# One core, attention, feed-forward and expert slots in one kernel: lower weight parts on GpSimd, fixed probability buffers, and a new order at slots 0 and 1

## The chip, the core and the metric

One core of a Trainium2 chip runs the whole kernel; the metric is the time of one execution on the device in microseconds. The engines are named as the profile names them: PE (TensorE, matmuls; PEld its weight loads), DVE (VectorE), ACT (ScalarE), POOL (GpSimd) and SP (SyncE, which here mostly issues transfers).

## The reference

Three stages follow each other. B=4, H=8, S=576, D=64, so there are 2304 tokens of width 512.

```python
scores = scale * np.matmul(q, k.transpose(0, 1, 3, 2))
scores = np.where(masks, scores, -1e9)          # heads 0-3 local (32 back), 4-7 strided by 32
attn = np.exp(scores - scores.max(-1, keepdims=True))
attn = attn / (attn.sum(-1, keepdims=True) + 1e-09)
x = (attn @ v) as rows of 512
xn = x / np.sqrt(np.mean(x * x, -1) + 1e-6) * rms_g
g = xn @ w_gate                                  # 512 -> 1536
x = (g * sigmoid(g) * (xn @ w_val)) @ w_out      # 1536 -> 512
e = argmax(x @ router + modality_bias[modality_id])
out = prob[e] * (relu(x @ w1[e]) @ w2[e])        # one of 8 experts a token, 512 -> 1024 -> 512
```

## The kernel before, in words

**Attention.** The work is cut into 48 units, 12 for each batch; unit u is two heads by a group of two to four tiles of queries. `attention(u, banks)` gives a unit four steps: `scores` (two matmuls a tile, then on DVE the scaled and masked scores go from PSUM into the SBUF tile `pr`, L207, and the row minimum is taken, L215; ACT takes the exponentials in place, L218), `norm` (DVE: row sum L238, reciprocal, product L242), `transpose` (PE L248, ACT copy L250) and `output` (PE L259). The first 12 units, those of batch 0, run alone at the start. In them the sum takes one column more than the probabilities, which holds 1e-9: GpSimd sets it in each unit (L185). The tile `pr` comes from a pool of three.

**Feed-forward.** Tokens are taken in nine chunks of 256. Before chunk 0 can start, its rows are squared and summed (L368 to L382), a reciprocal root is made on DVE (L388 to L396), and the normalised rows are split (L414 to L418). Every product is made of three matmuls, with both operands split into an upper and a lower part (`gate_val`, L512 to L514; `ff_out`, L537 to L539). The weights are 36 pieces of 128 by 512. They come as raw pairs of words, on ACT's transfer queue, and are made into two parts in three steps:

- `conv_a(n)`: GpSimd casts 16 bits of each word into one of two halves of `top` (L453);
- `conv_b(n)`: DVE shifts the other word and puts both together (L457);
- `conv_c(n)`: ACT rounds the result to the upper part (L464), DVE subtracts that from it for the lower part (L465).

The list `conv` holds the steps in the order a(0), b(0), a(1) with c(0), b(1), a(2) with c(1), and so on; `convert` takes them up while attention still runs. A scheduler with a simulated timeline sets each engine's order in this part of the program, so an edit can also move instructions that it doesn't name.

**Experts.** A router (`routes`, `route_i` for the last step of a chunk: four matmuls at L678 and one sum into `ids`) ranks the tokens of each expert. Slots of up to 256 tokens follow, each with one expert. `find`, `whose` and `count` work out which token columns and which expert each slot has; this is done at once for slots 1 and 2 (`SOON` is 2) and later for 13 more. For a slot t, `gather(t)` makes indices on DVE (L1046 to L1055) and issues two gathers of rows on POOL (L1058); `experts(t)` and `load` let SP fetch the expert's weights; `split(i)` halves them into upper (ACT L1074) and lower parts (DVE L1075); `x_transpose` puts the rows on PE (L1089) and splits them (L1093, L1094); `mm1` (L1110 to L1112) has four groups of two halves, `relu_split` makes `hT` (DVE L1127), `mm2` (L1140 to L1142) gives the output, and `finish(t)` scales it to `y` (DVE L1171 for its first half) and issues two scattered writes on POOL (L1172). This part stands in the order that the program gives (`manual_schedule`): slot 0 is written out by hand around the routing of the last chunk, and `run(1, BASE)` loops over the slots behind it.

Of the kernel before, what the change touches and what calls it, by code (L numbers as in the profile page):

```python
# [10 lines left out]
F32 = mybir.dt.float32  # L11
# [7 lines left out]
ALU = mybir.AluOpType  # L19
AX = mybir.AxisListType  # L20
# [33 lines left out]
def moe_kernel(  # L54
# [50 lines left out]
    pp = p_att.enter_context(tc.tile_pool(name="pp", bufs=4))  # L105
    xt_p = p_att.enter_context(tc.tile_pool(name="xt", bufs=4))

    def bank(tag, bufs=1):
        return ps.tile([128, 512], F32, tag=tag, name=tag, bufs=bufs)

# [61 lines left out]
    def attention(u, banks):  # L172

        b, p, g = units[u]
        local = p < 2
        n, t0, nq, nk = geometry(u)
        k0 = n * nq if local else n * nq + LQ - SQ
        st = {}

        def scores():  # L180
            t = qkv_t.pop((u, 0))

            pr = pp.tile([128, 4, LK + 1], F32, tag="pr", name="pr", bufs=3)
            if u < 12:
                G.memset(pr[:, :n, nk:nk + 1], 1e-9)  # L185
            mx = sm.tile([128, 4], F32, tag="mx", name="mx")
            sd = sm.tile([128, 4], F32, tag="sd", name="sd")
            sps = banks("s")
            if 0 < u < 12:
                fill(sps[:, 384:], 10)  # L190
            sps = sps[:, :4 * LK].rearrange("p (t k) -> p t k", k=LK)
            with close_to(pv_last):
                for i in range(n):
                    for h in range(2):
                        hp = slice(64 * h, 64 * h + 64)
                        T.matmul(
                            sps[hp, i, :nk],
                            t[hp, i * nq:i * nq + LQ],
                            t[hp, k0 + i * nq:k0 + i * nq + nk],
                            start=True,  # L200
                            stop=True,
                        )
            pv_last[0] = None
            first = 1 if local and g == 0 else 0
            for i0, i1, mask in ((0, first, m_loc0), (first, n, m_loc if local else m_str)):
                if i1 > i0:
                    V.scalar_tensor_tensor(  # L207
                        out=pr[:, i0:i1, :nk],
                        in0=sps[:, i0:i1, :nk],
                        scalar=-0.125,  # L210
                        in1=mask[:, :nk].unsqueeze(1).to_broadcast([128, i1 - i0, nk]),
                        op0=ALU.mult,
                        op1=ALU.add,
                    )
            V.tensor_reduce(out=mx[:, :n], in_=pr[:, :n, :nk], op=ALU.min, axis=AX.X)  # L215
            for i in range(n):
                pv = pr[:, i, :nk]
                act = A.activation(  # L218
                    out=pv,
                    in_=pv,  # L220
                    func=AF.Exp,
                    bias=mx[:, i:i + 1],
                    scale=-1.0,
                    accum_out=None if u < 12 else sd[:, i:i + 1],
                )
                if not flow_on:
                    mark[0] = act
            st["p"] = pr, sd
            if not 3 <= u < 6:
                load_part(0)  # L230
            if u < 4:
                load_part(1)

        def norm():
            pr, sd = st["p"]
            pv, sl = pr[:, :n, :nk], sd[:, :n]
            if u < 12:
                V.tensor_reduce(out=sl, in_=pr[:, :n, :nk + 1], op=ALU.add, axis=AX.X)  # L238
            else:
                V.tensor_scalar(out=sl, in0=sl, scalar1=1e-9, scalar2=None, op0=ALU.add)  # L240
            V.reciprocal(out=sl, in_=sl)
            V.tensor_tensor(out=pv, in0=pv, in1=sl.unsqueeze(2).to_broadcast([128, n, nk]), op=ALU.mult)  # L242

        def transpose():
            pr, _ = st.pop("p")
            pt = banks("t").rearrange("p (t k) -> p t k", k=128)
            for i in range(n):
                T.transpose(pt[:nk, i], pr[:, i, :nk], ident)  # L248
            ptS = st["t"] = pp.tile([128, 4, 128], F32, tag="ptS", name="ptS", bufs=2)
            A.copy(ptS[:nk, :n], pt[:nk, :n])  # L250

        def output():
            t = qkv_t.pop((u, 1))
            ptS = st.pop("t")
            ot = banks("o")
            with close_to([None]):
                for i in range(n):
                    for h in range(2):
                        pv_last[0] = T.matmul(  # L259
                            ot[64 * h:64 * h + 64, i * nq:(i + 1) * nq],  # L260
                            t[:nk, i, 64 * h:64 * h + 64],
                            ptS[:nk, i, 64 * h:64 * h + nq],
                            start=True,
                            stop=True,
                        )
            if local:
                x = x_t[b, p, g] = xt_p.tile([128, n * LQ], F32, tag=f"x{g}", name=f"x{g}", bufs=2)
                A.copy(x, ot[:, :n * LQ])
            else:
                if g == 0:  # L270
                    x_t[b, p] = xt_p.tile([128, S], F32, tag="xs", name="xs", bufs=4)
                x = x_t[b, p].rearrange("p (j c) -> p c j", c=CLS)
                c0, c1 = 3 * t0, min(3 * (t0 + n), CLS)
                A.copy(x[:, c0:c1], ot[:, :(c1 - c0) * LEN].rearrange("p (c j) -> p c j", j=LEN))
            if not 2 <= u < 8:
                load_part(1)
            n_out[0] = u + 1


        if local and b > 0:  # L280
            output.after = (S * (b - 1) + LQ * (t0 + n) - 1) // CH
        elif not local and b > 1:
            output.after = (S * (b - 1) - 1) // CH
        return scores, norm, transpose, output
# [176 lines left out]
    def conv_c(n):  # L461
        wk = raw_t.pop(n)[:, :, 0].bitcast(F32)
        w = w_t[n] = w_slot(n, [128, 2, 512], F32R, "wf")
        A.copy(w[:, 0], wk)  # L464
        V.tensor_tensor(out=w[:, 1], in0=wk, in1=w[:, 0].bitcast(F32), op=ALU.subtract)  # L465

    n_wl = [0]
    mark = [None]
# [784 lines left out]
    def run(t0, t1, first=False):  # L1253
# [9 lines left out]
                x_transpose(t0, q)  # L1263
        for t in range(t0, t1):
            ahead = t + 1 < t1
            if t + 2 < t1:
                gather(t + 2)
            if t - 1 in ys:
                finish(t - 1)
            ef = experts(t + 2) if ahead else None  # L1270
            if t == BASE - 1:
                half_pair(t, 0)
# [32 lines left out]
    with tc.manual_schedule():  # L1305
# [11 lines left out]
            next(ranks)  # L1317
        weave(ranks, route_g(j), tables())
        mm1(0, 2, (1,))
        mm1(0, 3, (0,))  # L1320
        route_i(j)
        mm1(0, 3, (1,), relu=False)
        gather(1)
        mm2(0, 0)
        weave(whose(0, SOON))
# [14 lines left out]
        for i in range(3, 7):  # L1340
            split(i)
        split(7)
        weave(find(SOON, NL))
        weave(whose(SOON, NL), count())
        ef = experts(2)
        for i in range(8):
            load(ef, i)
# [108 lines left out]
```

## Time and profile before

| | |
|---|---|
| median of three runs | 843.76 us (842.97 to 846.24) |
| the profiled execution | 844.88 us |
| its span | 843.0 us |
| granted TensorE clock, mean | 0.987 |
| busy PE / DVE / ACT / POOL | 820.0 / 520.6 / 381.5 / 88.1 us |

The span runs from the first to the last instruction in the trace; 1.9 us of the execution lie around it. A busy time is the sum of an engine's records, and records of one engine can overlap a little where an instruction starts before the one ahead has drained. The stretch up to about 46 us is attention of batch 0, with the first weight pieces; from there to 590 us the feed-forward runs, with attention of the other batches woven in; behind it come the expert slots.

### The profile page before, as it was taken

Reading aid. Unit: us, or ns where it says so; the run is one execution under the profiler, and the core shown is the slowest. Engines: PE = TensorE matmul, PEld = TensorE weight load, DVE = VectorE, ACT = ScalarE, POOL = GpSimd, SP = SyncE. Lnnn points to the kernel's source line nnn. Section 1 sums busy time; section 2 is a strip of 40 time slices with the busy share of each in tenths; the row PEclk is TensorE's granted clock in tenths of the full one; section 3 lists DMA queues with packets and bytes.
Section 4 is the critical chain, followed back from the end, with each engine's and each line's share of the span. In section 5 each row is a group of like instructions: output and inputs, shape, how many; then the busy total and the mean of one; then the engine's idle time right before and its main releaser. Section 6 shows DMA issues by size and latency. Waiting matters only on the chain.

```text
span 843.0 us, 17634 instructions
## 1 busy us (share of the span) xinstructions
PE 820.0 (97%) x6746; PEld 741.6 (88%) x6746; DVE 520.6 (62%) x1444; ACT 381.5 (45%) x943; POOL 88.1 (10%) x103
## 2 busy tenths in 40 slices
PE   8699999999999999999999999999999999999996
PEld 7588988988988998899989999999898999999995
DVE  5979994454663564653554525538589666666762
ACT  5756564343454345443242322325265555455552
POOL 2414410000000000000000000001023112221201
PEclk9879999999999999999999999999999999999998
DMA  9959301111211111200000000005159777777773
GB/s 249 365 190 344 107 25 34 29 34 39 63 57 43 38 34 51 76 23 1 26 11 26 1 1 27 1 26 214 37 175 338 224 225 229 217 232 230 230 222 111
DMA packets 35587, 96.99 MB, mean 115 GB/s; under 512 B 4786, under 2 KB 12322, under 8 KB 35496
## 3 DMA queue, kind: packets, MB, share of 16 engines
q1 hardware_dynamic: 26520, 67.08, 25.6%
q10 hardware_dynamic: 5616, 19.07, 6.1%
q0 software_dynamic: 3360, 9.64, 3.4%
q8 instruction: 55, 0.90, 0.4%
q14 instruction: 36, 0.29, 0.1%
HBM read 91.04 MB, written 9.71 MB: 120 GB/s over the span
## 4 chain that ended last, share of the span: by engine, by line
PE 77%; DVE 9%; issue 7%; DMA 4%; ACT 1%; POOL 1%; SPq 1%; POOLq 0%; DVEq 0%; ACTq 0%
PE gv L512 11%; PE gv L513 11%; PE gv L514 11%; PE o L538 5%; PE o L537 5%; PE o L539 5%; PE o L1140 3%; PE o L1142 3%; PE o L1141 3%; PE s L1110 2%; DVE raw L457 2%; PE s L1111 2%; PE s L1112 2%; PE mx L259 2%; DVE wf L465 2%
## 5 line engine op out<-in xcount | busy, mean ns | idle before, releaser
L512 PE MATMUL gv<-xh,wf 128*128 128x256 f32 x864 | 246.9, 287 | 0.6 <-DVE t L522 0.3
L513 PE MATMUL gv<-xl,wf 128*128 128x256 f32 x864 | 245.6, 285 | 0.3
L514 PE MATMUL gv<-xh,wf 128*128 128x256 f32 x864 | 245.0, 284 | 0.0
L512 PEld LDWEIGHTS gv<-xh,wf 128*128 128x128 f32 x864 | 163.4, 190 | 7.2 <-issue 1.2
L513 PEld LDWEIGHTS gv<-xl,wf 128*128 128x128 f32 x864 | 163.7, 189 | 5.0 <-DVE xl L418 0.9
L514 PEld LDWEIGHTS gv<-xh,wf 128*128 128x128 f32 x864 | 163.9, 190 | 0.5 <-issue 0.2
L1075 DVE TENSOR_TENSOR l<-stg,h 128x1024 fp32r<-128x1024 f32 x88 | 107.1, 1224 | 34.1 <-ACT h L1074 33.9
L1074 ACT CAST h<-stg 128x1024 fp32r<-128x1024 f32 x88 | 91.5, 1047 | 30.8 <-PE o L1142 14.5
L521 DVE SCALAR_TENSOR_TENSOR t<-t,gv 128x256 f32<-128x256 f32 x108 | 45.1, 418 | 85.8 <-ACT t L520 85.0
L520 ACT ACTIVATE t<-gv 128x256 f32<-128x256 f32 x108 | 41.1, 381 | 122.5 <-PE gv L514 111.7
L525 ACT CAST hh<-t 128x256 fp32r<-128x256 f32 x108 | 43.8, 406 | 76.5 <-DVE t L522 33.1
L537 PE MATMUL o<-wf,hh 128*128 128x512 f32 x192 | 77.0, 401 | 0.0
L538 PE MATMUL o<-wf,hh 128*128 128x512 f32 x192 | 76.2, 397 | 0.0
L539 PE MATMUL o<-wf,hl 128*128 128x512 f32 x192 | 74.9, 397 | 0.0
L526 DVE TENSOR_TENSOR hl<-t,hh 128x256 fp32r<-128x256 f32 x108 | 46.5, 431 | 33.8 <-ACT hh L525 32.7
L218 ACT ACTIVATE pr<-pr,mx 128x54 f32<-128x54 f32 (+1 forms) x160 | 52.3, 346 | 20.8 <-DVE mx L215 15.6
L1058 POOL DMA_INDIRECT xg<-rows_d,gi x22 | 24.7, 1122 | 300.3 <-DMA stg<-in 142.4
L1140 PE MATMUL o<-h,hT 128*128 128x512 f32 x128 | 51.9, 405 | 0.9 <-DVE y L1171 0.9
L1142 PE MATMUL o<-h,hT 128*128 128x512 f32 x128 | 50.1, 392 | 0.0
L1141 PE MATMUL o<-l,hT 128*128 128x512 f32 x128 | 49.8, 389 | 0.0
L522 DVE TENSOR_TENSOR t<-t,gv 128x256 f32<-128x256 f32 x108 | 45.1, 417 | 1.8
L1110 PE MATMUL s<-xh,h 128*128 128x256 f32 (+1 forms) x160 | 44.6, 279 | 0.0
(267 smaller groups left out, 1561.5 us busy)
## 6 DMA issues: line engine op xcount, KB each, us to landing
stg<-in SPq DMA_DIRECT2D x96, 512.0 KB
raw<-in ACTq DMA_DIRECT2D x36, 511.8 KB
rows_d<-x SPq DMA_DIRECT2D x18, 256.5 KB
qk<-in SPq DMA_DIRECT2D x14, 221.0 KB
qk<-in SPq DMA_DIRECT2D x8, 272.0 KB
qk<-in SPq DMA_DIRECT2D x8, 208.0 KB
v<-in SPq DMA_DIRECT2D x14, 108.0 KB
qk<-in SPq DMA_DIRECT2D x7, 167.0 KB
```

The costliest lines, as they stand in the source:

```text
L512: T.matmul(dst, wh[:, ks], xh[k], start=(k == order[0]), stop=False)
L513: T.matmul(dst, wh[:, ks], xl[k], start=False, stop=False)
L514: T.matmul(dst, wl[:, ks], xh[k], start=False, stop=(k == order[3]))
L537: T.matmul(o, h[:, ms], wh, start=(f == 0), stop=False)
L538: T.matmul(o, h[:, ms], wl, start=False, stop=False)
L539: T.matmul(o, l[:, ms], wh, start=False, stop=(f == NF - 1))
L1074: A.copy(h, lt["stg", i])
L1075: V.tensor_tensor(out=l, in0=lt["stg", i], in1=h.bitcast(F32), op=ALU.subtract)
L1110: T.matmul(dst, w[0][:, k, cs_], xh, start=(k == 0), stop=False)
L1140: T.matmul(ys[t][m], hh, w[0][:, c], start=(q == 0 and c == 0), stop=False)
L1141: T.matmul(ys[t][m], hh, w[1][:, c], start=False, stop=False)
L1142: T.matmul(ys[t][m], hl, w[0][:, c], start=False, stop=(q == 3 and c == 1))
```

## The change

It has four parts. The lower part of a weight piece n (`conv_c`) is made by GpSimd where n is odd and under 12, so for pieces 1, 3, 5, 7, 9 and 11. The probability tiles are three fixed ones, used by unit u modulo 3; their column 0 is set to 1e-9 once, at the start, and the probabilities lie in columns 1 to nk. In `run`, `finish(t - 1)` stands ahead of `gather(t + 2)`, and the late `find`, `count` and `whose` stand between them at t = 1, where they stood ahead of `experts(2)` before. In slot 0 both halves of the last `mm1` group stand ahead of `route_i`.

```diff
+    pr_t = [pp.tile([128, 4, LK + 1], F32, name=f"pr{i}", bufs=1) for i in range(3)]
+    for t in pr_t:
+        G.memset(t[:, :, 0:1], 1e-9)
...
-            pr = pp.tile([128, 4, LK + 1], F32, tag="pr", name="pr", bufs=3)
-            if u < 12:
-                G.memset(pr[:, :n, nk:nk + 1], 1e-9)
+            pr = pr_t[u % 3]
...
-                        out=pr[:, i0:i1, :nk],
+                        out=pr[:, i0:i1, 1:nk + 1],
...
-            pv, sl = pr[:, :n, :nk], sd[:, :n]
+            pv, sl = pr[:, :n, 1:nk + 1], sd[:, :n]
...
         A.copy(w[:, 0], wk)
-        V.tensor_tensor(out=w[:, 1], in0=wk, in1=w[:, 0].bitcast(F32), op=ALU.subtract)
+
+        (G if n < 12 and n % 2 else V).tensor_tensor(
+            out=w[:, 1], in0=wk, in1=w[:, 0].bitcast(F32), op=ALU.subtract
+        )
...
             ahead = t + 1 < t1
+            if t - 1 in ys:
+                finish(t - 1)
+            if t + 1 == SOON:
+                weave(find(SOON, NL), count())
+                weave(whose(SOON, NL))
             if t + 2 < t1:
                 gather(t + 2)
-            if t - 1 in ys:
-                finish(t - 1)
...
-        mm1(0, 3, (0,))
+        mm1(0, 3, relu=False)
         route_i(j)
-        mm1(0, 3, (1,), relu=False)
...
-        weave(find(SOON, NL))
-        weave(whose(SOON, NL), count())
```

Line numbers below are each version's own; the changed one's are 2 to 5 higher. On POOL, at the start (`top` is the cast's result, `raw` a raw piece, `wf` a piece's two parts), the order was

```order
L453 CAST top<-raw 128x512
L185 MEMSET pr 128x3
L185 MEMSET pr 128x4
L453 CAST top<-raw 128x512
L185 MEMSET pr 128x4
L453 CAST top<-raw 128x512 x2
L185 MEMSET pr 128x3
L453 CAST top<-raw 128x512 x2
L185 MEMSET pr 128x3
L453 CAST top<-raw 128x512 x2
L185 MEMSET pr 128x2
```

and is now

```order
L455 CAST top<-raw 128x512 x4
L468 ISA
L468 TENSOR_TENSOR wf<-raw,wf 128x512
L455 CAST top<-raw 128x512 x2
L468 TENSOR_TENSOR wf<-raw,wf 128x512
L455 CAST top<-raw 128x512 x3
L468 TENSOR_TENSOR wf<-raw,wf 128x512
L455 CAST top<-raw 128x512
L468 TENSOR_TENSOR wf<-raw,wf 128x512
L455 CAST top<-raw 128x512 x2
L468 TENSOR_TENSOR wf<-raw,wf 128x512
L455 CAST top<-raw 128x512 x2
```

The memsets between the casts are gone, subtractions stand between them, and an instruction marked ISA, which has no operands, stands ahead of the first of these.

On DVE in the same stretch (around the shift-and-ors of pieces 3 and 4, L457 before and L459 now) the order was

```order
L242 TENSOR_TENSOR pr<-pr,sd 128x4x96
L457 SCALAR_TENSOR_TENSOR raw<-raw,top 128x512
L238 TENSOR_REDUCE sd<-pr 128x4
L215 TENSOR_REDUCE mx<-pr 128x3
L465 TENSOR_TENSOR wf<-raw,wf 128x512
L457 SCALAR_TENSOR_TENSOR raw<-raw,top 128x512
```

and is now

```order
L244 TENSOR_TENSOR pr_103<-pr_103,sd 128x4x96
L217 TENSOR_REDUCE mx<-pr_105 128x3
L459 SCALAR_TENSOR_TENSOR raw<-raw,top 128x512
L240 TENSOR_REDUCE sd<-pr_104 128x4
L240 TENSOR_REDUCE sd<-pr_105 128x3
L209 SCALAR_TENSOR_TENSOR pr_103<-s_611,cs 128x3x96
L243 RECIPROCAL sd<-sd 128x4
L468 TENSOR_TENSOR wf<-raw,wf 128x512
L243 RECIPROCAL sd<-sd 128x3
L217 TENSOR_REDUCE mx<-pr_103 128x3
L244 TENSOR_TENSOR pr_104<-pr_104,sd 128x4x96
L459 SCALAR_TENSOR_TENSOR raw<-raw,top 128x512
```

Three rows stood between the two shift-and-ors, and now eight stand there; the subtraction of piece 2 (L465, now L468) is among them in either list.

On DVE at the seam of slots 0 and 1 (`w`, `s_l`, `et`, `ei` are of the late `find` and `whose`, `pick`, `pz` and `gi` of `gather`, `y` of `finish`, `hT` of slot 1), the end of the late find, the gather and `finish` stood as

```order
L1018 TENSOR_SCALAR more<-cf 128x1
L1004 TENSOR_SCALAR et<-et,m 128x13
L1008 CAST ei<-et 128x13
L1010 TENSOR_TENSOR ei<-et 128x13
L1046 SCALAR_TENSOR_TENSOR pick_7490<-iota,s_l,ids 128x144
L1050 TENSOR_REDUCE pz_7491<-pick_7490 128x2
L1052 TENSOR_SCALAR pz_7491<-pz_7491 128x2
L1055 SCALAR_TENSOR_TENSOR gi<-pz_7491 128x2
L1171 TENSOR_SCALAR y_8279<-o_8101,go_7483 128x512
L1127 SCALAR_TENSOR_TENSOR hT<-s_8307,hT 128x2x64
L1127 SCALAR_TENSOR_TENSOR hT<-s_8307,hT 128x2x128
```

and now, from the last splits of slot 1's weights on,

```order
L1080 TENSOR_TENSOR l<-stg,h 128x1024 x5
L1176 TENSOR_SCALAR y_8202<-o_8047,go_7429 128x512
L984 TENSOR_TENSOR w_7458<-excl,place 128x208
L1021 TENSOR_REDUCE cf<-wd 128x1
L986 TENSOR_TENSOR w_7459<-incl,place 128x208
L1023 TENSOR_SCALAR more<-cf 128x1
L988 TENSOR_TENSOR w_7458<-w_7458,w_7459 128x208
L990 SCALAR_TENSOR_TENSOR w_7459<-u,w_7458 128x208
L992 TENSOR_REDUCE s_l<-w_7459 128x13
L994 SCALAR_TENSOR_TENSOR s_l<-place,s_l 128x13
L1001 TENSOR_TENSOR w_7459<-w_7458,e_l 128x208
L1005 TENSOR_REDUCE et<-w_7459 128x13
```

`y` has moved from behind the find and the gather to ahead of both; `hT` stands behind all of them in either version.

## Rows read from the trace of the kernel before

**Rows 1.** The page, parts 1 and 4: busy time, and the chain that ended last.
```profile
PE 820.0 (97%) x6746; PEld 741.6 (88%) x6746; DVE 520.6 (62%) x1444; ACT 381.5 (45%) x943; POOL 88.1 (10%) x103
...
PE 77%; DVE 9%; issue 7%; DMA 4%; ACT 1%; POOL 1%; SPq 1%; POOLq 0%; DVEq 0%; ACTq 0%
```

**Rows 2.** The chain of waits, 0 to 120 us: start, us, what.
```profile
9.77 5.95 DMA raw<-in
15.74 7.78 DMA raw<-in
...
46.10 0.80 PE gv L512 x2
```

**Rows 3.** Table by stage: columns PE, PEld, DVE, ACT, POOL, granted clock, DMA share, GB/s.
```profile
24.40:37.00 12.60, 7.41 (x119) 5.64 (x116) 12.56 (x27) 10.62 (x30) 7.16 (x12) 0.94 1.03 396
...
46.10:53.00 6.90, 6.90 (x42) 6.35 (x43) 3.58 (x9) 2.82 (x14) 0.00 (x0) 0.53 0.16 46
...
70.00:110.00 40.00, 39.97 (x352) 36.78 (x351) 39.68 (x84) 22.84 (x64) 16.58 (x19) 1.00 0.52 192
110.00:120.00 10.00, 8.94 (x82) 7.88 (x81) 9.97 (x22) 7.07 (x21) 1.94 (x2) 1.00 0.13 37
```

**Rows 4.** DVE's timeline, 24 to 42.6 us: start, us, line, operation, tiles.
```profile
28.14 0.68 DVE L465 TENSOR_TENSOR wf<-raw,wf 128x512 fp32r<-128x512 f32 x1
28.74 1.19 DVE L457 SCALAR_TENSOR_TENSOR raw<-raw,top 128x512 int32<-128x512 int32 x1
...
37.00 0.68 DVE L368 TENSOR_TENSOR sq<-sq 128x512 f32<-128x512 f32 x1
...
38.19 0.41 DVE L369 TENSOR_TENSOR sq<-sq 128x256 f32<-128x256 f32 x1
```

**Rows 5.** DVE's groups by form, 24.4 to 42.6 us: busy us, mean ns.
```profile
L242 DVE TENSOR_TENSOR pr<-pr,sd 128x288 f32<-128x288 f32 x2 | 0.9, 448 | 0.0
L242 DVE TENSOR_TENSOR pr<-pr,sd 128x192 f32<-128x192 f32 x2 | 0.7, 354 | 0.0
```

**Rows 6.** POOL's timeline, 10 to 40 us.
```profile
25.42 1.02 POOL L453 CAST top<-raw 128x512 f16<-128x512 bf16 x1 [1.01 <-DMA raw<-in]
26.35 0.10 POOL L185 MEMSET pr<- 128x3 f32 x1
...
28.49 0.96 POOL L453 CAST top<-raw 128x512 f16<-128x512 bf16 x1 [0.48 <-DMA raw<-in]
...
33.82 1.46 POOL L453 CAST top<-raw 128x512 f16<-128x512 bf16 x1 [0.78 <-DMA raw<-in]
...
35.83 0.76 POOL L453 CAST top<-raw 128x512 f16<-128x512 bf16 x1 [0.55 <-DVE raw L457]
```

**Rows 7.** PE's timeline around the seam of slots 0 and 1; waits in brackets.
```profile
609.45 0.51 PE L678 MATMUL mx<-ab 128*128 128x144 bf16 x2 [0.39 <-DVE ab L666]
...
611.27 0.40 PE L1140 MATMUL o<-h,hT 128*128 128x512 f32 x1
...
620.80 0.60 PE L1089 MATMUL pt<-cs,xg 128*128 128x128 f32 x4
...
634.80 0.47 PE L1140 MATMUL o<-h,hT 128*128 128x512 f32 x1 [0.88 <-DVE y L1171]
```

**Rows 8.** DVE's timeline around the seam.
```profile
617.32 3.50 DVE L1075 TENSOR_TENSOR l<-stg,h 128x1024 fp32r<-128x1024 f32 x3 [2.00 <-ACT h L1074]
621.94 0.56 DVE L1094 TENSOR_TENSOR xl<-pt,xh 128x384 fp32r<-128x384 f32 x1 [1.13 <-ACT xh L1093]
...
629.65 0.37 DVE L979 TENSOR_TENSOR w<-excl,place 128x208 f32<-128x208 f32 x1
...
633.91 0.74 DVE L1171 TENSOR_SCALAR y<-o,go 128x512 f32<-128x512 f32 x1
```

**Rows 9.** POOL's timeline around the seam.
```profile
616.04 0.96 POOL L1058 DMA_INDIRECT xg<-rows_d,gi  x1 [0.30 <-issue]
```

**Rows 10.** DMA issues, 610 to 625 us: line, count, median us to landing.
```profile
xg<-rows_d,gi POOLq DMA_INDIRECT x3, 3.4
```

More of the change, by code (lines that the diff above doesn't have):

```diff
@@ L214, in scores @@
                     )
-            V.tensor_reduce(out=mx[:, :n], in_=pr[:, :n, :nk], op=ALU.min, axis=AX.X)
+            V.tensor_reduce(out=mx[:, :n], in_=pr[:, :n, 1:nk + 1], op=ALU.min, axis=AX.X)
             for i in range(n):
-                pv = pr[:, i, :nk]
+                pv = pr[:, i, 1:nk + 1]
                 act = A.activation(
@@ L247, in transpose @@
             for i in range(n):
-                T.transpose(pt[:nk, i], pr[:, i, :nk], ident)
+                T.transpose(pt[:nk, i], pr[:, i, 1:nk + 1], ident)
             ptS = st["t"] = pp.tile([128, 4, 128], F32, tag="ptS", name="ptS", bufs=2)
```

## The prediction

> **What bounds the kernel now.** I read the page first: TensorE (PE) is busy 820.0 of 843.0 us, and the chain that ended last is 77% PE and 9% VectorE (DVE) [rows 1]. So a change off PE pays only where PE waits. The edits touch two such places: the start, and the seam between the expert slots 0 and 1.
>
> The chain of waits over the start comes second. It runs through two transfers of raw weight pieces (5.95 and 7.78 us), a GpSimd (POOL) cast, and then DVE; PE carries it from 46.10 us, with the first gate matmul [rows 2]. The table by stage says why: between 24.40 and 37.00 us DVE is busy 12.56 of 12.60, POOL 7.16, PE 7.41; from 46.10 to 53.00 PE is full, and so it is from 70 to 110 us, 39.97 of 40.00 [rows 3]. So DVE time saved before about 42 us moves everything behind it, and PE covers what is saved later. Between 110 and 120 us PE is busy 8.94 of 10.00 [rows 3]: a microsecond can come from there, hardly more.
>
> TensorE's clock is granted at 0.94 from 24.40 to 37.00 us, where PE is thin, and at 0.53 from 46.10 to 53.00 [rows 3], that is near the 1.2 GHz level while the first gate matmuls run back to back. A shorter start could move that, so it is a rival below.
>
> **The lower parts on GpSimd.** A subtraction costs DVE 0.60 us net: it starts at 28.14 and the next instruction at 28.74, though 0.68 is shown, since records overlap by 0.08 [rows 4]. Of the five that stood ahead of the first square (old L368, at 37.00 us [rows 4]) the new DVE order keeps two: 3 x 0.60 = 1.80 us less. But the scheduler pulled other work into the gap: two products by the reciprocals, 0.45 and 0.35 shown [rows 5], 0.37 and 0.27 net, a row minimum and a row sum of the smaller width, some 0.25 each, and small ones, together about 1.35. That leaves 0.45. Between the two squares 1.19 us passed (37.00 to 38.19 [rows 4]); the new order has about 0.34 less there. Sum: **-0.8 us** on DVE if nothing else changes.
>
> What GpSimd's subtraction takes is in no row. With one input of 128 by 512 a cast takes 0.76 us undisturbed and 1.46 disturbed [rows 6]. Two inputs bound it by 0.76 below and by twice that, 1.52, above; I take the middle, 1.15.
>
> DVE also pays for POOL. Two instructions with two inputs from on-chip memory and the same size stand side by side in the timeline: the subtraction at 28.14 takes 0.68 us, the shift-and-or at 28.74 takes 1.19 [rows 4], with POOL's cast running from 28.49 to 29.45 [rows 6]. That is 0.51 lost to one cast; the other way round a cast grew to 1.46. Such losses sum to about 1.0 us for the nine casts of this stretch (an estimate). For the three or four subtractions that now join them, each longer than a cast, I add 0.5 us. The ends: nothing, when they fall beside DVE work with one input, and 0.6 for each of four, 2.4, when each starts just ahead of a two-input instruction. The start so gives -0.8 + 0.5 = **-0.3 us**, from -0.8 to +1.6.
>
> The Trainium skill, "SBUF — State Buffer", section Who interferes with whom, says that a VectorE instruction with two on-chip inputs and a GpSimd instruction that reads on-chip memory shut each other out, the later one for the whole of the first. The rows of 1.19 and 1.46 agree. By that rule the move loses as soon as each subtraction holds DVE for over 0.60 us, and by "GPSIMD Engine Reference", section 3.1 (2.6 cycles an element for two inputs), it would last about 1.1 us (an estimate); the sum would then be that of the second rival.
>
> Pieces 7, 9 and 11 move too, but their lower parts come after 46 us, where PE is full: 0, with ±1.0 from the idle time up to 120 us [rows 3].
>
> **The probability buffers.** Twelve one-column memsets of 0.10 us [rows 6] go from POOL and three come, at the very start. They lay in POOL's idle time, ahead of a cast at worst: -0.1. A column's shift leaves sizes and counts alike, and the buffers rotated over three before, so no wait for a free one is new: 0.
>
> **Slot 0.** Before, PE did half of the last gate group, then the four matmuls of the routing indices, with a wait of 0.39 us for DVE ahead of the second pair, then the second half, and began the output matmuls at 611.27 us [rows 7]. Now all 24 gate matmuls come first. The second half (12 matmuls, between that pair at 609.45 and 611.27) runs into the waits, so the output matmuls start about 1.4 us sooner. But not all of that carries. The transposes of slot 1's input, old L1089 at 620.80 us [rows 7], need the gathered rows: the second gather is issued at 616.04 for 0.96 us [rows 9] and lands 3.4 us after issue in the median [rows 10], at 619.4, or 620.4 counted from its end. And DVE's three weight splits end at 617.32 + 3.50 = 620.82; the lower part of slot 1's input started at 621.94, after 1.13 idle [rows 8]. So the DVE chain behind it moves by 0.4 to 1.1 us. I take **-0.8**; nothing if the splits of slot 1's weights are held by their transfers.
>
> **Slot 1 and later.** The 13 instructions of the late find (from 629.65, 3.2 us) go behind the result y at 633.91 [rows 8], which ended PE's wait of 0.88 us at 634.80 [rows 7]. But hT, right behind y on DVE, still has the same work ahead, and the next matmuls need it: the wait goes to hT. 0.1 at best: I take 0. The output transfers now stand ahead of the gather of slot t+2 on POOL's queue; that gather is wanted a slot later: 0. SP's queue keeps its order, paced by the same splits.
>
> **Sum.** -0.3 - 0.1 - 0.8 = -1.2, with 0.1 kept for rounding **-1.1 us**. The profiled execution took 844.88 us, so 843.8 by it; it lies 1.1 above the median of the runs, 843.76, and medians are compared: **842.7 us**, 0.13% less. A measurement of this kernel tells about 0.5% (4.2 us) from no change, so this is a forecast of no change.
>
> **The rivals.** *Slower: code that must be brought in.* The new POOL stream has an instruction without operands, marked ISA, right ahead of its first subtraction, as at the program's start; no row shows what it takes. Call it R. The cast of piece 3 ends at 25.42 + 1.02 = 26.44 [rows 6]; behind it come R, the subtraction of 1.15 and the cast of piece 4, some 0.95, which ends at 28.5 + R. DVE wants it at 28.74 by the old order [rows 4]; in the new one eight instructions stand between the shift-and-ors of pieces 3 and 4 where three stood, so at about 29.9. The stall is R - 1.4, and the whole turns slower from R = 2.5. Should R be a transfer in this stretch, where the DMA engines are full (share 1.03 [rows 3]), its nearest rows are the raw pieces of 5.95 and 7.78 us [rows 2]: +4.6 or +6.4 on DVE, 847.3 to 849.1 in all. For it: nothing near could hide 6 us. Against: an ISA row opens the old program too, and POOL's later rows show nothing of it. Chance 0.17. The Trainium skill's "GPSIMD Engine Reference", section 2.1, gives 5.95 us for the first call to freshly loaded code; by it, 847.3.
>
> *Each subtraction blocks DVE.* Four times 0.6 in place of 0.5 in all: +1.9, 844.6; with 1.52 us each, 845.5. POOL then has 7.16 + 4 x 1.15 = 11.8 of 12.60 us and is near a bound itself. Chance 0.18.
>
> *Faster: the clock.* If a denser start leaves PE's clock up, the matmuls from 46.10 to 53.00 take 6.90 x 0.47 = 3.2 us less: 839.5, and 838.7 with the start at -0.8 and the seam at -1.1. Against: nothing in the edits feeds PE before 37 us. Chance 0.10.
>
> *The seam gives nothing*, where the gathers hold the transposes: 843.5, inside the forecast's range.
>
> **How the numbers follow.** Forecast 0.55, own range 841.0 to 844.4 (the seam from -1.1 to 0, the start from -0.8 to +0.4, the later work ±1.0). With the rivals at 0.18, 0.17 and 0.10 the range of 840.3 to 848.2 leaves out the clock's case and the upper half of the slow one, some 0.19. Faster by over 0.5% (below 839.5): the clock and a tail, 0.12. Slower (above 848.0): the upper half of R and a tail, 0.13. Same: 0.75.
>
> **What would show it.** Right: no subtraction on POOL over 1.6 us, DVE full to about 42 us, the first gate matmul near 45.8, the transposes before the end of the splits, PE's wait on y gone and one on hT of about 0.8 in its place. Microseconds of idle DVE behind the ISA row would show the slow rival; more rows of 1.1 us and over among the two-input DVE instructions, the second; a granted clock near 1.00 at 46 us, the third. I am wrong if the first gate matmul is off 45.8 by over 2 us, or the seam by over 1.

## The result, and the profile after

The changed kernel takes **852.17 us** in the median of 4 runs (852.07 to 852.34); the kernel before took 843.94 in the 4 runs beside it (842.97 to 846.24). The ratio is 1.0089, interval 1.0072 to 1.0106: slower by 8.2 us between the medians and by 7.5 us by the ratio, beyond the 0.5% that the prediction set as a bound, and outside its range.

To see where, I cut both traces at three points: the first GpSimd cast (the first raw piece has landed; over all the profiles here that is between 14.1 and 18.4 us), the first gate matmul, and the first transposes of slot 0.

| us | before | after | difference |
|---|---|---|---|
| start: first cast to first gate matmul | 30.32 | 33.76 | +3.4 |
| middle: to the first transposes of slot 0 | 545.10 | 549.46 | +4.4 |
| end: to the end of the span | 251.8 | 250.7 | -1.1 |
| whole span | 843.0 | 850.1 | +7.1 |

The missing 0.4 is the later first cast. So the seam gave what was forecast, and the loss has two places: the start, and one in the middle where the prediction had put nothing.

From the page after: busy time, and the costliest groups, with what ended PE's idle time ahead of them in the last columns.
```profile
PE 821.0 (97%) x6746; PEld 743.4 (87%) x6746; DVE 524.6 (62%) x1438; ACT 380.8 (45%) x943; POOL 100.8 (12%) x100
...
L1145 PE MATMUL o<-h,hT 128*128 128x512 f32 x128 | 52.0, 406 | 0.0
L1147 PE MATMUL o<-h,hT 128*128 128x512 f32 x128 | 50.3, 393 | 1.1 <-DVE hT L1132 1.1
```
PE's busy time hardly moved from [rows 1], POOL's grew by 12.7 us. Of the seam, the output matmuls' wait for `y` is gone (0.0 at L1145), and 1.1 us on `hT` stand there instead, now on L1147.

**The start.** The table by stage after, in the columns of [rows 3]:
```profile
24.40:37.00 12.60, 7.95 (x129) 6.04 (x128) 11.91 (x28) 10.49 (x31) 8.48 (x8) 1.00 1.03 400
...
42.60:46.10 3.50, 0.37 (x2) 0.00 (x0) 3.19 (x13) 1.01 (x2) 1.32 (x1) 0.50 0.00 0
46.10:53.00 6.90, 5.86 (x47) 5.02 (x48) 5.18 (x14) 4.91 (x19) 0.00 (x0) 0.50 0.23 67
...
70.00:110.00 40.00, 36.71 (x317) 34.11 (x316) 38.05 (x76) 22.39 (x68) 16.95 (x20) 0.91 0.55 195
110.00:120.00 10.00, 10.00 (x96) 9.21 (x95) 10.00 (x20) 5.57 (x13) 3.93 (x4) 1.00 0.14 41
```
At 46.10 us, where PE was full before, it had just spent 3.5 us with 0.37 of work. POOL was busy 8.48 of 12.60 (7.16 before). PE's timeline, from 40 and from 74 us on, with waits in brackets, shows the first gate matmul and two waits of the middle:
```profile
49.92 0.80 PE L517 MATMUL gv<-xh,wf 128*128 128x256 f32 x2 [0.73 <-ACT xh L419]
...
77.93 0.51 PE L250 MATMUL mx<-cs,pr 128*54 128x128 f32 x3 [1.48 <-ACT xs L276]
80.26 0.58 PE L517 MATMUL gv<-xh,wf 128*128 128x256 f32 x1 [1.81 <-DVE t L527]
```
The first gate matmul stands at 49.92; it was at 46.10 [rows 2]. What held it shows when POOL's and DVE's timelines are read side by side. POOL's subtractions (start, us, line, tiles):
```profile
25.44 0.77 POOL L455 CAST top<-raw 128x512 f16<-128x512 bf16 x1 [0.93 <-DVE sd L243]
26.22 1.49 POOL L468 TENSOR_TENSOR wf<-raw,wf 128x512 fp32r<-128x512 f32 x1
...
30.91 2.23 POOL L468 TENSOR_TENSOR wf<-raw,wf 128x512 fp32r<-128x512 f32 x1 [1.36 <-ACT wf L466]
...
37.76 1.71 POOL L468 TENSOR_TENSOR wf<-raw,wf 128x512 fp32r<-128x512 f32 x1
...
44.43 1.32 POOL L468 TENSOR_TENSOR wf<-raw,wf 128x512 fp32r<-128x512 f32 x1 [4.11 <-DVE nt L396]
```
And DVE's instructions of the same moments:
```profile
26.84 1.42 DVE L459 SCALAR_TENSOR_TENSOR raw<-raw,top 128x512 int32<-128x512 int32 x1
...
35.45 0.69 DVE L468 TENSOR_TENSOR wf<-raw,wf 128x512 fp32r<-128x512 f32 x1 [0.62 <-ACT wf L466]
...
38.24 1.44 DVE L244 TENSOR_TENSOR pr<-pr,sd 128x192 f32<-128x192 f32 x1
39.61 1.19 DVE L370 TENSOR_TENSOR sq<-sq 128x512 f32<-128x512 f32 x1
...
44.43 0.16 DVE L397 TENSOR_TENSOR nt<-nt,na 128x2 f32<-128x2 f32 x1
44.62 1.14 DVE L398 SCALAR_TENSOR_TENSOR nr<-nt,nr 128x2 f32<-128x2 f32 x1
```
The ISA row cost nothing: the cast ahead of it ends at 25.44 + 0.77 = 26.21, and the subtraction starts at 26.22. But the shift-and-or at 26.84 took 1.42 us instead of 0.68, the product at 38.24 took 1.44 instead of 0.35, and an instruction on two columns at 44.62 took 1.14, while its twin just ahead took 0.16. Each ends no more than its own usual time behind the subtraction beside it, which ends at 26.22 + 1.49 = 27.71, 37.76 + 1.71 = 39.47 and 44.43 + 1.32 = 45.75; DVE's three end at 28.26, 39.68 and 45.76. The square at 39.61 (37.00 before [rows 4]) took 1.19 in the same way, beside the cast that POOL began at 39.42. The other way round, the subtraction at 30.91 grew to 2.23. Up to the first square such excess sums to 3.0 us on DVE, against some 1.0 in the trace of before; behind it to another 1.5, and 0.62 go to a wait for ACT at 35.45. That pays for the three subtractions that DVE got rid of, and more.

**The middle.** Four stretches of 4 us after, same columns as the table by stage:
```profile
72.00:76.00 4.00, 4.00 (x58) 3.81 (x57) 3.90 (x10) 1.66 (x7) 2.25 (x3) 1.00 0.11 26
76.00:80.00 4.00, 0.97 (x7) 0.48 (x6) 3.96 (x11) 2.22 (x8) 1.22 (x2) 0.84 0.66 207
80.00:84.00 4.00, 3.74 (x17) 3.74 (x18) 3.97 (x10) 3.58 (x13) 1.89 (x3) 0.50 1.03 420
84.00:88.00 4.00, 4.00 (x24) 3.73 (x23) 2.93 (x8) 1.21 (x3) 1.41 (x2) 0.80 0.88 323
```
Before, PE is full from 70 to 110 us at a clock of 1.00 [rows 3]. Now it idles for 3.0 us from 76 to 80 us: 1.48 waiting for `xs` and 1.81 for `t`, the second of the two DVE instructions of that name behind a gate product, in PE's timeline above. The first wait goes back to DVE as well: `xs` is an ACT copy, and it stood in ACT's queue behind a cast that had waited 1.27 us for DVE, up to 76.64. Then the granted clock is 0.50, the 1.2 GHz level, for the next stretch and 0.80 for the one behind. Idle 3.0 + 0.3, and (1 - 0.50) x 3.74 + (1 - 0.80) x 4.00 = 2.7 at the lower clock, are 6.0 us of PE; 1.1 come back at 110 to 120 us, full now and 8.94 before [rows 3]. DVE's timeline shows why `t` was late:
```profile
63.72 0.41 DVE L527 TENSOR_TENSOR t<-t,gv 128x256 f32<-128x256 f32 x1
...
71.34 2.17 DVE L797 CAST mf<-md 128x18 f32<-128x18 int32 x1
...
79.79 0.41 DVE L527 TENSOR_TENSOR t<-t,gv 128x256 f32<-128x256 f32 x1
```
From one `t` at 63.72 to the next at 79.79 DVE let 16.1 us pass; up to 125 us the longest such time before is 8.1 (95.38 to 103.49). In its instruction order 29 stand between the first of those rows and the next `t` of either kind, at 78.58; before, up to 125 us, there were never more than 13. The scheduler put them there. A long run by itself is nothing new: further on, the kernel before has one of 33 instructions and 13.3 us, and every version has one like it.
```profile
234.82 0.41 DVE L522 TENSOR_TENSOR t<-t,gv 128x256 f32<-128x256 f32 x1
...
248.08 0.42 DVE L522 TENSOR_TENSOR t<-t,gv 128x256 f32<-128x256 f32 x1
```
There many are instructions on two columns, PE never waits for `t`, it loses about 1 us in all to a wait for ACT, and the clock stays at 1.00. Back in the change, between 63.72 and 79.79, a cast of the routing flags, 18 columns, 0.17 us before, took 2.17: POOL did these two meanwhile.
```profile
71.42 1.34 POOL L468 TENSOR_TENSOR wf<-raw,wf 128x512 fp32r<-128x512 f32 x1
72.67 0.80 POOL L455 CAST top<-raw 128x512 f16<-128x512 bf16 x1
```

### The profile page after: what moved, and what is told of

Same layout as the page of the kernel before. It is cut to its first block, busy times and chain, and to the rows that moved or that the text cites. A ratio compares the mean times of both kernels' runs of the same rounds, so it can differ in the third digit from the quotient of the medians.

```text
span 850.1 us, 17603 instructions
## 1 busy us (share of the span) xinstructions
PE 821.0 (97%) x6746; PEld 743.4 (87%) x6746; DVE 524.6 (62%) x1438; ACT 380.8 (45%) x943; POOL 100.8 (12%) x100
## 5 line engine op out<-in xcount | busy, mean ns | idle before, releaser
L1079 ACT CAST h<-stg 128x1024 fp32r<-128x1024 f32 x88 | 91.5, 1047 | 32.8 <-PE o L1147 14.5
L1145 PE MATMUL o<-h,hT 128*128 128x512 f32 x128 | 52.0, 406 | 0.0
L1147 PE MATMUL o<-h,hT 128*128 128x512 f32 x128 | 50.3, 393 | 1.1 <-DVE hT L1132 1.1
L1063 POOL DMA_INDIRECT xg<-rows_d,gi x22 | 27.4, 1244 | 183.1 <-DMA stg<-in 142.7
```

What stands on the lines that cost most here:

```text
L1079: A.copy(h, lt["stg", i])
L1145: T.matmul(ys[t][m], hh, w[0][:, c], start=(q == 0 and c == 0), stop=False)
L1147: T.matmul(ys[t][m], hl, w[0][:, c], start=False, stop=(q == 3 and c == 1))
```

## The experiments

Three suspects: GpSimd's reads shut DVE out, the new instruction order starves PE, and the fixed buffers are not free. In the table, start, middle and end are cut as above, and the last two columns, for 50 to 125 us, are the most DVE instructions between two rows of `t`, and the longest time from one second `t` to the next.

| kernel | median us | ratio, interval | start | middle | end | DVE rows | longest us |
|---|---|---|---|---|---|---|---|
| before | 843.94 | | 30.32 | 545.10 | 251.8 | 13 | 8.1 |
| the change | 852.17 | 1.0089 (1.0072 to 1.0106) | 33.76 | 549.46 | 250.7 | 29 | 16.1 |
| e1: the change, all subtractions on DVE | 846.28 | 1.0032 (1.0019 to 1.0046) | 32.45 | 544.50 | 250.3 | 15 | 9.5 |
| e2: before, only the subtractions moved | 853.48 | 1.0115 (1.0091 to 1.0139) | 33.77 | 550.09 | 251.4 | 29 | 16.2 |
| e3: before, only the new seam | 844.08 | 1.0000 (0.9984 to 1.0016) | 29.99 | 544.63 | 250.4 | 13 | 8.1 |
| e4: the change, pieces 1, 3, 5 alone on GpSimd | 846.41 | 1.0035 (1.0016 to 1.0053) | 32.94 | 544.26 | 250.6 | 13 | 8.1 |
| e5: before, only the fixed buffers | 846.78 | 1.0022 (1.0010 to 1.0035) | 32.60 | 544.90 | 251.6 | 15 | 9.5 |
| e6: the change, pieces 7, 9, 11 alone on GpSimd | 847.70 | 1.0044 (1.0030 to 1.0059) | 32.69 | 545.52 | 250.4 | 23 | 13.0 |
| e7: before, with extra GpSimd reads | 850.86 | 1.0078 (1.0057 to 1.0098) | 34.25 | 547.82 | 251.4 | 13 | 8.3 |
| e8: before, with extra GpSimd memsets | 845.32 | 1.0013 (0.9993 to 1.0033) | 30.66 | 545.47 | 251.9 | 12 | 8.0 |
| e9: the change, piece 11 back on DVE | 854.01 | 1.0109 (1.0092 to 1.0126) | 33.07 | 551.78 | 250.5 | 33 | 17.1 |
| e10: the change, the flags' cast on ACT | 849.86 | 1.0057 (1.0040 to 1.0073) | 33.61 | 546.89 | 250.5 | 26 | 14.1 |
| e11: e3 with twice the filler matmuls | 852.95 | 1.0102 (1.0085 to 1.0119) | 36.6 | 544.92 | 250.4 | 15 | 9.5 |
| e12: the change, memsets for the subtractions | 845.98 | 1.0024 (1.0012 to 1.0036) | 30.78 | 547.80 | 250.5 | 31 | 14.5 |

A ratio is against the runs of the kernel before on the same chip (medians 843.94 to 844.58), so I compare kernels by their ratios, times 844 us. A median is of 4, 9 or 10 runs; the cuts are of one profiled execution each, which for most lies within 1 us of the median, but 3.1 below it for e1, 1.9 below for e6 and 1.4 to 1.5 above for e12 and e9.

**One part undone, one part alone.** e1 gives the subtractions back to DVE:

```diff
-        (G if n < 12 and n % 2 else V).tensor_tensor(
+        V.tensor_tensor(
```

> The change with all lower parts made by DVE again; fixed probability buffers and the new seam stay. Theory 1 (the subtractions on GpSimd cost all of the loss, the rest gains a little): first gate matmul near 46.1 us, total about 843, some 9 us under the change. Rival (the buffers or the seam share the loss, for instance by another order that the scheduler makes): well above 844, and the first gate matmul later than 46.1.

e2 is the kernel before with nothing but the subtractions on GpSimd:

```diff
-        V.tensor_tensor(out=w[:, 1], in0=wk, ...
+        (G if n < 12 and n % 2 else V).tensor_tensor(out=w[:, 1], in0=wk, ...
```

> The kernel before with only the six lower parts moved to GpSimd. Theory 1: at least as slow as the change and about 1 us over it, 852 to 854, since the seam's gain is missing; first gate matmul near 50 us and a PE gap of some 3 us near 78. Rival (moves and fixed buffers act together): 845 to 849.

e3 is the kernel before with nothing but the new order at slots 0 and 1 (the diff's last four pieces):

> The kernel before with only the new order at slots 0 and 1. My term for the seam: -0.8 us, so 843.0 to 843.3, everything up to 590 us as before, and PE's wait of 0.88 us on y gone with one on hT in its place. Rival (the gathered rows hold the transposes): no change, 843.9.

e5 is the kernel before with nothing but the fixed probability buffers (the diff's first pieces):

> The kernel before with only the three fixed probability buffers. My term: -0.1 us, so 844 and everything in place. Rival (the buffers change the scheduler's order or the rotation and cost about 2 us, which would explain why the change without GpSimd's subtractions came out at 846.3 in the median): 845.5 to 847, with the first gate matmul or the stage behind it later than before.

The subtractions alone give the whole loss (e2, 1.0115, with the start of the change and a middle 0.6 longer), and without them (e1, 1.0032 for 1.0089) 4.8 us are gone. Not all: e1 and e5 stay above the kernel before by intervals that leave out 1, and both start 2.1 to 2.3 us later. So the fixed buffers, which I had costed at nothing, cost 1.9 us in e5, and the rival of either run was right. e5's PE timeline and its table by stage show how:
```profile
33.48 1.09 PE L250 MATMUL pt<-cs,pr 128*96 128x128 f32 x4 [2.24 <-DVE pr L244]
...
48.71 0.58 PE L517 MATMUL gv<-xh,wf 128*128 128x256 f32 x1
```
```profile
32.00:34.00 2.00, 0.52 (x3) 0.50 (x4) 2.00 (x4) 1.33 (x4) 1.07 (x1) 0.50 1.05 412
```
The product by the reciprocals that the first transposes of a unit wait for comes later in the new DVE order; the transposes start at 33.48 after a wait of 2.24 us, where they started at 31.24 before, and the clock is at 0.50 from 32 us (before, from 36). Why the scheduler sets another order when only the buffers change was not tried. e2, without the fixed buffers, starts as late as the change with them: the two costs of the start do not add.

The seam: e3 shows no change in its total, and in the trace -1.4 us. All nine kernels with the new seam end in 250.3 to 250.7 us, all five with the old in 251.4 to 251.9. So it is worth 1.1 us, too small for a total of this kernel to show.

**Early or late pieces.** e4 leaves on GpSimd only the subtractions of pieces 1, 3 and 5, e6 only those of 7, 9 and 11:

```diff
-        (G if n < 12 and n % 2 else V).tensor_tensor(
+        (G if n < 6 and n % 2 else V).tensor_tensor(         # e4
+        (G if 6 < n < 12 and n % 2 else V).tensor_tensor(    # e6
```

> The change with only pieces 1, 3 and 5 on GpSimd; 7, 9 and 11 go back to DVE. Theory 1a (each subtraction blocks DVE where it stands, so the losses add): the start keeps its loss of about 3 us, the gap near 78 us goes, total 845 to 847. Theory 1b (the late gap follows from the late start, not from pieces 7 to 11): the gap stays, 850 to 852.

> The change with only pieces 7, 9 and 11 on GpSimd; 1, 3 and 5 go back to DVE. Theory 1a (losses add where the subtractions stand): the first gate matmul at 46 to 47 us, the PE gap near 76 us and the second fall of the clock there, total 848 to 850. Theory 1b (the late gap comes only with a late start): no gap, 844 to 846.

e4 came out as theory 1a says, with a start 0.5 us above e1's and no loss in the middle. Over e1, the early ones alone cost 0.3 us, the late ones alone 1.0 (the intervals overlap, so neither is told from nothing), both together 4.8. By e4 the exchange at the start is about even: what DVE saves it waits. e6 fell between what the theories gave: its longest run of DVE instructions is 23, PE lost some 1.1 us around 74 us, and the clock stayed at 1.00.

**The reads by themselves.** e7 is the kernel before, all its work kept, with a GpSimd subtraction of constants into an unused tile beside each of the six pieces; e8 has two memsets of about the same length there, which read nothing.

```diff
         V.tensor_tensor(out=w[:, 1], in0=wk, ...
+        if n < 12 and n % 2:                       # scr: 128 by 1024, made once
+            A.copy(scr[:, 0:1], w[:, 0, 0:1].bitcast(F32))
+            c = cs.rearrange("p a c -> p (a c)")
+            G.tensor_tensor(out=scr[:, :512], in0=c[:, :512], in1=c[:, 128:], op=ALU.subtract)  # e7
+            G.memset(scr, 0.0); G.memset(scr[:, :512], 0.0)                                     # e8
```

> The kernel before, all lower parts on DVE, and for each of pieces 1, 3, 5, 7, 9 and 11 one more GpSimd subtraction of 128 by 512 of two constant tiles into a spare tile that nothing reads (with a one-column ACT copy that ties its place in time). It reads on-chip memory, but the weight pieces wait for it nowhere except in GpSimd's own queue. Theory 2 (GpSimd's reads shut DVE out): DVE instructions of over 1 us beside each, first gate matmul 2 to 4 us late, total 849 to 854. Rival (the loss comes from the lower part being late for whoever waits for it): 844 to 846.

> The same as the run with the extra reading subtraction, but the extra work is two GpSimd memsets of 1024 and 512 columns, about as long (0.95 + 0.5 us) and without any read. Theory 2 (GpSimd's reads shut DVE out): DVE's durations as before, 844 to 845.5. Rival (GpSimd's queue is full and its casts come late, whatever it does): as slow as the run with the reading subtraction.

Both came out as theory 2 says. This is the cleanest pair: the order between gate products stays as before (13 and 12 instructions), and the reads cost 1.0078, the memsets nothing that can be told (1.0013). The start is 3.6 us longer with reads than with memsets. The order of DVE's first rows is not quite the same in the two, but the lost time can be counted row by row: from the first cast to the first gate matmul, what DVE's instructions took above the shortest of their form sums to 5.2 us in e7, 0.8 in e8 and 1.1 before. DVE's timeline in e7, and POOL's under it:
```profile
25.79 1.76 DVE L457 SCALAR_TENSOR_TENSOR raw<-raw,top 128x512 int32<-128x512 int32 x1
...
36.95 1.75 DVE L368 TENSOR_TENSOR sq<-sq 128x512 f32<-128x512 f32 x1
...
43.11 1.22 DVE L395 TENSOR_TENSOR nt<-nt,na 128x2 f32<-128x2 f32 x1
```
```profile
25.58 1.42 POOL L471 TENSOR_TENSOR scr<-cs 128x512 f32<-128x512 f32 x1
...
36.70 1.45 POOL L471 TENSOR_TENSOR scr<-cs 128x512 f32<-128x512 f32 x1
...
43.05 1.26 POOL L471 TENSOR_TENSOR scr<-cs 128x512 f32<-128x512 f32 x1 [1.87 <-ACT scr L469]
```
The same pairing as in the change: 1.76 us for a shift-and-or, 1.75 for a square, 1.22 for an instruction on two columns, each beside a GpSimd subtraction. The groups by form from 24.4 to 46 us (busy us, mean ns), e7 and then e8:
```profile
L457 DVE SCALAR_TENSOR_TENSOR raw<-raw,top 128x512 int32<-128x512 int32 x5 | 5.0, 991 | 0.0
```
```profile
L457 DVE SCALAR_TENSOR_TENSOR raw<-raw,top 128x512 int32<-128x512 int32 x6 | 4.2, 696 | 0.0
```
Shift-and-ors of one form take 991 ns in the mean beside reads and 696 beside memsets. The Trainium skill, "SBUF — State Buffer", section Who interferes with whom, says that a DVE instruction with two on-chip inputs contends with a GpSimd instruction that reads on-chip memory, and not with one that only writes it; both halves agree with these two runs. e7's middle lost 2.7 us too: PE idled 1.17 us from 64 to 68 (0.83 waiting for ACT's `xs`, 0.34 for DVE's `hl`, none for `t`) and had a clock of 0.50 and 0.69 in the two stretches behind. So reads alone can open a gap in the middle, with the old order.

**One bad instruction?** I then held that the flags' cast, shut out for 2.17 us right ahead of the gap, made the middle's loss. e9 takes the last subtraction, which shut it out, back to DVE; e10 lets ACT do that cast:

```diff
-        (G if n < 12 and n % 2 else V).tensor_tensor(
+        (G if n < 10 and n % 2 else V).tensor_tensor(    # e9
...
-        V.tensor_copy(mf[:, :, 1], md[:, :, 0])
+        A.copy(mf[:, :, 1], md[:, :, 0])                 # e10
```

> The change with piece 11's lower part back on DVE; 1, 3, 5, 7 and 9 stay on GpSimd, and DVE's order is the change's up to 70 us. Theory 3 (the gap of PE near 76 us and the clock's second fall start where one GpSimd instruction, the subtraction of piece 11 and the cast behind it, hold DVE's cast of the modality flags for 2.17 us): no gap, clock 1.00 from 70 to 110 us, total 847 to 849. Rival (all late subtractions share it): 850 to 852, a gap of over 2 us in the same place.

> The change with all six lower parts on GpSimd; only the cast of the modality flags, the DVE instruction that took 2.17 us beside the subtraction of piece 11, is made by ACT. Theory 3 (what decides is that this one DVE instruction is shut out, with everything queued behind it): the gap near 76 us shrinks to under 1 us, total 847 to 849.5. Rival (another instruction is shut out in its place): a wait of 1.3 us or more on DVE beside the same subtraction, and 850 to 852.

e9 missed whatever was expected of it: 854.01, the slowest of all, with no shut-out of the cast. Its PE timeline and its table by stage:
```profile
83.37 0.58 PE L517 MATMUL gv<-xh,wf 128*128 128x256 f32 x1 [4.76 <-DVE t L527]
```
```profile
76.00:80.00 4.00, 2.54 (x42) 2.02 (x42) 3.97 (x11) 2.13 (x6) 1.42 (x2) 1.00 0.36 103
80.00:84.00 4.00, 0.63 (x3) 0.63 (x4) 4.00 (x9) 2.76 (x13) 1.52 (x2) 0.70 0.86 299
84.00:88.00 4.00, 4.00 (x20) 4.00 (x20) 4.00 (x9) 1.98 (x6) 1.86 (x2) 0.50 1.03 415
```
A single wait of 4.76 us for `t`, behind a run of 33 DVE instructions and 17.1 us, and again the clock at 0.50 behind it. In e10 the next DVE instruction on the same flags took the blow:
```profile
71.61 1.95 DVE L798 TENSOR_SCALAR mf<-mf 128x18 f32<-128x18 f32 x1
```
Its gap is still there (a PE wait of 2.2 us for `t`), and its total lies between the two that were expected. It gained 2.7 us on the change, with a shorter run (26) as well, so it doesn't tell the two causes apart. The theory of one bad instruction fell with e9.

**The order without the reads.** e12 is the change with the six GpSimd subtractions replaced by three memsets of the lower part each, so POOL is as busy and DVE as relieved, but only its casts still read:

```diff
-        (G if n < 12 and n % 2 else V).tensor_tensor(
-            out=w[:, 1], in0=wk, in1=w[:, 0].bitcast(F32), op=ALU.subtract
-        )
+        if n < 12 and n % 2:
+            for _ in range(3):
+                G.memset(w[:, 1].bitcast(F32), 0.0)
+        else:
+            V.tensor_tensor(out=w[:, 1], in0=wk, in1=w[:, 0].bitcast(F32), op=ALU.subtract)
```

> The change, but in place of each of the six GpSimd subtractions three memsets of the lower part (512 columns each, about 1.5 us together): the lower parts of pieces 1, 3, 5, 7, 9 and 11 are left out, as zeros. GpSimd then reads nothing there, while the scheduler's DVE order keeps the long run of 31 instructions between two posts of a gate (29 in the change, at most 13 before). Theory 4 (two causes: at the start GpSimd's reads shut DVE out; the gap near 76 us comes from that long run in DVE's order): the first gate matmul at 44 to 47 us, the gap of 2 us and more on DVE's posts is still there and the clock falls after it, total 845 to 849. Rival (both losses come from GpSimd's reads): no gap, 841 to 844.

It separates the causes as expected, with the first gate matmul at 47.33, 0.3 above its bound. The start falls to 30.78, 3.0 below the change and 1.7 below e1: that is about what the shut-out costs, and about what relieving DVE would bring without it, in one profile each (e7 against e8 gave 3.6 for the first). Both are rough, since DVE's order at the start is not the same in the three, and an order alone made 2.1 to 2.3 us in e1 and e5. The rows bear out the first: DVE's excess, summed as for e7, is 4.6 us in the change and 2.8 in e12, of which 1.2 lie in three one-input instructions on two columns, beside memsets. DVE's first of these, and the memsets on POOL:
```profile
40.76 0.66 DVE L392 TENSOR_SCALAR nr<-na 128x2 int32<-128x2 int32 x1
```
```profile
40.41 1.57 POOL L470 MEMSET wf<- 128x512 f32 x3
```
The same instruction took 0.17 us in the change. The middle of e12 still loses 2.7 us:
```profile
76.70 0.39 PE L519 MATMUL gv<-xh,wf 128*128 128x256 f32 x1 [2.03 <-DVE t L529]
```
```profile
72.00:76.00 4.00, 2.67 (x23) 2.40 (x21) 4.00 (x10) 2.07 (x7) 0.77 (x1) 1.00 0.48 122
76.00:80.00 4.00, 3.30 (x17) 3.30 (x18) 3.93 (x11) 2.94 (x12) 1.68 (x2) 0.65 1.01 405
```
31 DVE instructions between two `t`, a PE wait of 2.03 for it, and a clock of 0.65. So the order opens the gap without a single shut-out by a subtraction. Its order is near the change's but not the same (31 and 29), so 2.7 is no exact share of the 4.4. What goes with the loss, in the table, is the longest time between two `t`: 13.0 us in e6 with +0.4 in the middle, 14.1 in e10 with +1.8, 14.5 in e12 with +2.7, 16.1 in the change with +4.4, 16.2 in e2 with +5.0 and 17.1 in e9 with +6.7. The order lengthens it (e12), and so does what is shut out inside it (the flags' cast in the change, 2.0 us longer). e7 alone lost over 1 us without such a time.

**A denser start for PE.** For the rival on the clock, e11 is e3 with twice the filler matmuls ahead of the first gate product:

```diff
-        fill(sps[:, 384:], 10)
+        fill(sps[:, 384:], 20)
```

> A version that may beat both: the kernel before with the new seam alone, and 20 in place of 10 filling matmuls ahead of the scores of units 1 to 11 (their result is not used). If PE's thin stretch is what lets the clock fall at 34 to 36 us, a fuller PE keeps it near 1.00 up to 46 us: 838 to 842. Rival (the stretch stays too thin, or the filling delays the scores on PE): 843 to 846.

A miss: the start took 36.6 us, 6.6 more than e3, the first gate matmul moved to 55.01, and ahead of it, from 46.10 to 55 us, the clock was at 0.50 all the same. The filler did change the clock before that (0.87 from 42.60 to 46.10, where e3 has 0.50), so the rival on the clock is not ruled out, only this way of using it. Where the 6.6 us come from was not followed up.

Of these versions none beat the kernel before; e3 equals it.

## Why the prediction was wrong

- **What bounds it:** right where it says that a change off PE pays only where PE waits. Wrong was the turn of it, that PE "covers" what happens behind 46 us. It covers DVE time as long as the gate products' `t` come in time, and 39.97 of 40.00 said nothing of how much later they might come.
- **The later pieces, 0 ±1.0:** this step failed most. The middle lost 4.4 us. e12 shows that the order loses 2.7 without the subtractions' reads, e7 that reads lose as much in the old order; in both PE idles for 1 to 2 us, for `t` in e12 and for `xs` and `hl` in e7, and a stretch near the 1.2 GHz level follows. How the two share the change's 4.4 stays open, as they don't add: early alone +0.3, late alone +1.0, both +4.8 in all. The instruction order could be read beforehand: 29 DVE instructions between two `t` instead of 13; their time was for the run to show, as the 33 at 234.82 us cost little. I compared the order at the start and the seam, not there.
- **GpSimd's subtraction, 1.15 us:** measured 1.49, 2.23, 1.71, 1.32, 1.47 and 1.34. Even the shortest is above the estimate, most are within its bound of 1.52. The Trainium skill's "GPSIMD Engine Reference", section 3.1, has 2.6 cycles an element for two inputs, about 1.1 us here (an estimate); the trace disagrees, and the measurement decides.
- **The shut-out, 0.5 us, ends 0 and 2.4:** the mechanism was named and the size was wrong. The change against e12 puts it at about 3.0 us of the start, above the upper end. (The 1.0 us that the prediction gives for the casts of before is borne out, but 24.40 to 37.00 us hold seven of them, not nine.) I had counted four subtractions of 0.6 each; but two-input DVE instructions stand so close together that nearly every POOL read meets one, small instructions are held as long as large ones, and casts that are moved meet others.
- **Relieving DVE, -0.8:** too small. Without reads (e12) the start is 1.7 shorter than in e1, about the three subtractions' 1.80. How much the work pulled forward cost is not shown, since the order changed too.
- **The probability buffers, -0.1:** wrong in sign and size, +1.9 (e5). I costed the memsets and the column, not the new order.
- **Slot 0, -0.8:** right, -1.1. Slot 1, 0: right, `y`'s wait went to `hT`. In DVE's and PE's timelines of the seam:
```profile
625.39 3.50 DVE L1080 TENSOR_TENSOR l<-stg,h 128x1024 fp32r<-128x1024 f32 x3 [2.01 <-ACT h L1079]
628.80 0.55 DVE L1099 TENSOR_TENSOR xl<-pt,xh 128x384 fp32r<-128x384 f32 x1
...
636.50 0.75 DVE L1176 TENSOR_SCALAR y<-o,go 128x512 f32<-128x512 f32 x1
...
641.49 0.61 DVE L1132 SCALAR_TENSOR_TENSOR hT<-s,hT 128x128 fp32r<-128x128 f32 x2
```
```profile
627.47 0.60 PE L1094 MATMUL pt<-cs,xg 128*128 128x128 f32 x4
```
The transposes start at 627.47, ahead of the end of the splits (625.39 + 3.50 = 628.89), and the lower part follows at 628.80 with no wait, where it had 1.13 [rows 8].
- **The range:** the ends of the prediction's own range, without its rivals, don't come out of the terms. The start was given up to +1.6 but entered with +0.4, and the terms as entered add up to 840.9 to 845.2, not 841.0 to 844.4. Even with +1.6 the upper end would be 846.4.
- **The rivals:** code to be brought in cost nothing at that place (26.21 to 26.22). The rival on blocking, chance 0.18, had the right mechanism and the right sign at 844.6 to 845.5, though only for the start, and short by some 7 in all. The clock came in on the other side from the one I gave it: lost in the middle, not won at the start.

## What to carry to other kernels

When an edit gives work to another engine, read the new instruction order of the engines that it relieves over the whole program, and look for the longest time between two instructions that PE waits for. A full PE is no cover once that time is too long: here 13 us cost little and 14 to 17 us cost 1.8 to 6.7. A gap can be paid again at a lower clock behind it, as in the change, e7, e9 and e12; in e6, after 1.1 us of idle PE, it was not. GpSimd is a poor place for two-input work beside a DVE that is full of two-input instructions: beside the DVE time saved, price what it takes from DVE (here 3.0 to 3.6 us for four subtractions of 5.5 to 6.8 us together). Work there that only writes cost nothing that a total shows (e8), though it too held small one-input instructions in e12.

## What the runs showed of the hardware that was not expected

- A shut-out does not scale with the instruction that is held. One on two columns took 1.14 us in the change and 1.22 in e7, 0.16 alone.
- One-input instructions can be held too, through two GpSimd instructions in a row: the cast of 18 columns took 2.17 us in the change (0.17 before) beside a subtraction of 1.34 and the cast of 0.80 behind it, and its follower 1.95 in e10. The section Who interferes with whom of the Trainium skill's "SBUF — State Buffer" says that copies, casts and `tensor_scalar` can take the read and write port pair that DVE shares with GpSimd; these two rows agree.
- For such instructions a GpSimd instruction that only writes can be enough: in e12 three `tensor_scalar` instructions on two columns, one behind the other, took 0.66, 0.55 and 0.48 us beside three memsets, and 0.16 to 0.17 each in the change.
- GpSimd's memsets in the same place, about 1.5 us for each of six pieces in e8, held nothing that a total shows (1.0013, interval 0.9993 to 1.0033).
